# Batch 1's second softmax and first layer in one piece instead of two, with the order of the work searched anew

## The chip, the cores and the metric

The kernel runs on one core of one Trainium2 chip. The metric is the device time of one execution in microseconds; the median of a few runs is given. The profile shows one execution of the program, and its span runs from the first to the last instruction on the core.

## What is computed

An attention in two steps over 8 batches with 8 heads, 576 tokens and a head size of 64, in which 32 packed queries per head first gather the keys and values and the tokens then attend to the 32 gathered rows, and a two-layer network with a squared relu on the 4608 x 512 result (x). w_in is 512 x 2048 and w_out 2048 x 512.

```python
def sm_attn(qq, kk, vv):
    s = scale * np.matmul(qq, kk.transpose(0, 1, 3, 2))
    s = s - np.max(s, axis=-1, keepdims=True)
    a = np.exp(s)
    a = a / (np.sum(a, axis=-1, keepdims=True) + 1e-09)
    return np.matmul(a, vv)
p_packed = sm_attn(p, k, v)
out = sm_attn(q, p_packed, p_packed)
...
h = x @ w_in
r = np.maximum(h, 0.0)
g = r * r
return (g @ w_out).astype(np.float32)
```

## The kernel before, in words

The work goes batch by batch (b = 0 to 7), with 4 heads packed into the 128 partitions, so that each batch has two "quads" of heads (`qd`). For each batch:

- k is loaded, transposed (piece `Tk`, L741) and multiplied with p (`S1`, L774); its softmax is taken (`MX` L793, `EX` L801), transposed and multiplied with v (`PV`, L821), normalised (`XN`, L830), and transposed (`XQ`, `XM`, `XC`). This gives the packed rows.
- The packed rows are multiplied with w_in beforehand (`M`, L851, evicted by `MC`, L647 or L649), so that the second attention's output and the first layer need one product only: a2 (the softmax of the second scores) times M.
- q is loaded and transposed (`Tq`, L738) and multiplied with the packed rows (`S2`, L868) into PSUM. The second softmax works on a layout where the 32 columns of a token lie in a row: transposition out of PSUM (`SI`, L889), maximum (`SM`, L895), subtraction (`SU`, L899), exponential on ScalarE (`SE`, L902), sum and reciprocal (`SS`, L905 and L906), multiplication (`SN`, L912), transposition into a2 (`SO`, L916). All of these but `SE` are on VectorE.
- The first layer is M times a2: 16 blocks of 128 features. A relu from PSUM into bf16 and a square into gT follow, each on ScalarE or VectorE as the planner chooses.
- The second layer takes tiles of 128 tokens. Tiles 0 to 8 (and 13, 22 and 31) are plain sums over the 16 blocks (`F2`, L979; 31 is `FZ`, L997); the others are done in groups of four tiles by a Strassen step (`GP`, L1046), with sums of the weights (`WS`, L1024, eight instructions in all) and of the activations (`GS`, L1031) formed on VectorE. Tiles 0 to 3 need batch 0 alone, tile 4 needs batches 0 and 1, tiles 5 to 8 need batch 1.

Two batches differ from this. `PARTS` (L573) cuts the tokens of a batch for the second softmax and the first layer. A part is a pair: how many times 32 tokens it has, and how many feature blocks one first-layer group takes.

```python
PARTS = {0: ((4, 4), (6, 4), (8, 2)), 1: ((8, 2), (10, 2))}
def parts(b):
    return PARTS.get(b, ((8, 0), (10, 0)))
```

Batch 0 has parts of 128, 192 and 256 tokens. Batch 1 has parts of 256 and 320 tokens. A batch that is in `PARTS` takes each step from `SM` to `SO` once for every part (`SN` even once per quad of heads), and its first layer once for every part (pieces `F.1.x.j`, `R.1.x.j`, `Q.1.x.j`; `fh_mm` L953, `fh_relu` L961 or L963, `fh_sq` L971 or L973; two feature blocks to a group). A batch that is not in it takes the softmax over all 576 tokens at once (`steps`, L1177) and the first layer in 16 blocks of two times 288 tokens (pieces `F1`, `R`, `SQ`; `f1_mm` L925, `f1_relu` L935 or L937, `f1_sq` L943 or L945, the square over two blocks at a time). The score matmuls `S2` and the transposition `SI` are in two parts (256 and 320 tokens) for batches 1 to 4 either way; batches 5 to 7 use a DMA transposition and another form.

The order is set by a planner (`Plan.forward`, L70) that runs when the program is built. Every piece has an engine (or a choice of ScalarE and VectorE), an assumed duration, pieces that it waits for, and PSUM or buffer slots that it takes. The planner steps through an assumed time; whenever an engine is free, it starts the ready piece with the smallest priority. The priority is the level of the piece in the code (10 b + 2 for the second softmax of batch b, 30 + 10 t / 4.5 for second-layer tile t, 45 for the weight sums) plus a number from the table `TABLE['o']`; `TABLE['l']` shifts the choice between ScalarE and VectorE. Each engine then executes its instructions in the planned order. Before the first second-layer matmul, idle time that the plan sees on TensorE is filled with dummy matmuls (`keep_clock`, L653), which keep the clock up.

The loads run in a fixed order (`ORDER`) on the GpSimd queue, eight in flight at a time: the ninth is issued when the first has landed. Only batch 0's k, the p rows of batches 2 to 7 (L673, issued behind `XQ.1`) and the stores use the SyncE queue; the first p rows use ScalarE's. Batch 2's first scores `S1.2` need those p rows (`P.1` L680, `PT.1` L683).

PSUM has three pairs of banks (`PAIRS`) for scores, M and first-layer blocks, and four single banks for transpositions and second-layer tiles.

Of the kernel before, what the change touches and what calls it, by code (L numbers as in the profile page):

```python
# [14 lines left out]
P = 128  # L15
# [26 lines left out]
class Plan:  # L42
# [185 lines left out]
TABLE = {'o': {'Lk.0.0i': 134.746555333, 'Lk.0.1i': 23.540356465, 'Lk.0.0': 2.551236235, 'LP.0': 181.100529118,  # L228
# [330 lines left out]
def kernel_impl(tc, q, k, v, p, w_in, w_out, out):  # L559
    nc = tc.nc  # L560
    B, H, S, Dh = q.shape
# [11 lines left out]
    PARTS = {0: ((4, 4), (6, 4), (8, 2)), 1: ((8, 2), (10, 2))}  # L573
# [866 lines left out]
```

## Time and profile before

| | us |
|---|---|
| median of 3 runs (lowest, highest) | 236.37 (235.14, 236.86) |
| the profiled execution | 235.5 |
| its span | 233.7 |
| TensorE busy, 95% of the span | 221.5 |
| VectorE busy, 85% | 199.0 |
| ScalarE busy, 65% | 150.8 |
| GpSimd busy, 24% | 56.7 |

The profiled execution is 0.9 us under the median and within the three runs. A busy TensorE is not TensorE at its peak, since matmuls overlap and their ends are modelled; what is read below are its idle times and the spacing of matmuls. A row that gives "idle before" names what ended the wait. Where a row stands for several instructions, its count is behind the x.

### The profile page before, as it was taken

What the parts mean: (1) busy time and instruction counts of PE and PEld (TensorE: products, weight loads), DVE (VectorE), ACT (ScalarE), POOL (GpSimd) and SP (SyncE); (2) the same over time, 40 slices, a digit from 0 to 9 for tenths busy, and PEclk for the clock granted to TensorE, in tenths of its full rate; (3) what the DMA queues carried; (4) which work ended last, traced back from release to release, by engine and by line L of the source; (5) the groups of instructions that cost most, each with busy time, mean ns of one, the idle gap of its engine ahead of it and who ended that gap; (6) DMA issues with size and microseconds to landing.
All of it is one profiled execution on the core that took longest, in us unless ns stands there. A gap on an engine that the chain in (4) does not pass through costs nothing.

```text
span 233.7 us, 6367 instructions
## 1 busy us (share of the span) xinstructions
PE 221.5 (95%) x2615; PEld 159.8 (68%) x2631; DVE 199.0 (85%) x333; ACT 150.8 (65%) x246; POOL 56.7 (24%) x101
## 2 busy tenths in 40 slices
PE   8868999999999999999999999999999999999991
PEld 5644675455554467678767877887678878888880
DVE  3659887998899989999999999999999999479330
ACT  3334985388675888983997847749977917295100
POOL 9774445333344655630000000000000000000000
PEclk9999999999999999999999999999999999999998
DMA  6999999999999999999962969654241006106125
GB/s 234 189 150 206 205 207 203 202 204 262 221 224 214 228 229 194 174 134 153 207 140 63 157 78 210 157 101 97 56 92 45 1 3 147 36 0 140 42 56 168
DMA packets 46620, 34.06 MB, mean 146 GB/s; under 512 B 25280, under 2 KB 38336, under 8 KB 46592
## 3 DMA queue, kind: packets, MB, share of 16 engines
q0 software_dynamic: 19360, 18.03, 48.7%
q1 hardware_dynamic: 26384, 15.11, 30.2%
q10 hardware_dynamic: 848, 0.52, 1.0%
q8 instruction: 20, 0.33, 0.5%
q14 instruction: 8, 0.07, 0.1%
HBM read 37.22 MB, written 9.44 MB: 200 GB/s over the span
## 4 chain that ended last, share of the span: by engine, by line
PE 73%; DMA 21%; POOL 2%; issue 1%; DVE 1%; ACT 0%; POOLq 0%
PE ps L1046 32%; PE ps L925 21%; PE ps L979 9%; DMA w_out_b<-in_moe_w_out_dram 8%; DMA kq_b<-in_q_dram 6%; DMA w_in_b<-in_moe_w_in_dram 3%; PE ps L851 3%; DMA v_b<-in_v_dram 3%; PE ps L953 2%; PE ps L997 2%; PE ps L821 1%; PE ps L868 1%; PE ps L807 1%; PE ps L774 1%; POOL v_b L662 1%
## 5 line engine op out<-in xcount | busy, mean ns | idle before, releaser
L935 ACT ACTIVATE r_b<-ps 128x576 bf16<-128x576 f32 x84 | 49.5, 659 | 14.9 <-PE ps L925 14.7
L925 PE MATMUL ps<-a,M 128*128 128x288 bf16 x384 | 52.6, 286 | 0.2
L925 PEld LDWEIGHTS <-M 128*128 128x128 bf16 x384 | 37.2, 98 | 11.2 <-DVE a L916 0.3
L979 PE MATMUL ps<-w_out_b,gT 128*128 128x512 bf16 x160 | 41.3, 379 | 0.9 <-issue 0.3
L1046 PEld LDWEIGHTS <-gT 128*128 128x128 bf16 x384 | 36.7, 98 | 7.5 <-issue 3.1
L647 ACT CAST M<-ps 128x1024 bf16<-128x1024 f32 (+1 forms) x33 | 29.4, 932 | 16.5 <-PE ps L851 16.4
L1046 PEld LDWEIGHTS <-gS 128*128 128x128 bf16 x288 | 27.8, 98 | 4.1 <-DVE gS L1031 0.4
L991 POOL DMA_DIRECT2D out_dram<-o_sb x2 | 1.1, 571 | 120.1 <-DVE o_sb L1066 119.0
L945 DVE TENSOR_TENSOR gT<-r_b 128x1152 bf16<-128x1152 bf16 x38 | 27.8, 750 | 2.1 <-ACT r_b L935 2.0
L1066 DVE TENSOR_TENSOR o_sb<-o_sb,ps 128x512 f32<-128x512 f32 x30 | 20.2, 674 | 10.1 <-PE ps L1046 10.1
L647 ACT COPY o_sb<-ps 128x512 f32<-128x512 f32 (+1 forms) x24 | 13.7, 573 | 21.4 <-PE ps L997 9.5
L979 PEld LDWEIGHTS <-gT 128*128 128x128 bf16 x176 | 16.2, 98 | 14.7 <-issue 1.7
L1046 PE MATMUL ps<-w_out_b,gT 128*128 128x256 bf16 x192 | 24.1, 273 | 0.0
L1046 PE MATMUL ps<-wS,gT 128*128 128x256 bf16 x192 | 23.6, 273 | 0.0
L1046 PE MATMUL ps<-wS,gS 128*128 128x256 bf16 x192 | 23.6, 273 | 0.0
L953 PE MATMUL ps<-a,M 128*128 128x256 bf16 (+3 forms) x160 | 19.1, 262 | 1.4 <-DVE a L916 0.5
L953 PEld LDWEIGHTS <-M 128*128 128x128 bf16 x160 | 13.7, 98 | 7.3 <-issue 1.4
L961 ACT ACTIVATE r_b<-ps 128x512 bf16<-128x512 f32 (+2 forms) x28 | 16.9, 645 | 2.6 <-PE ps L953 2.5
L801 ACT ACTIVATE e<-ps,n 128x576 bf16<-128x576 f32 x16 | 11.8, 739 | 7.3 <-DVE n L793 7.2
L653 PE MATMUL ps<-o_sb 128*128 128x256 bf16 x90 | 13.5, 312 | 1.1 <-DVE o_sb L656 1.1
L793 DVE TENSOR_REDUCE n<-ps 128x1 f32<-128x576 f32 x16 | 11.6, 748 | 1.9 <-PE ps L774 1.9
L851 PE MATMUL ps<-w_in_b,ppT 64*32 64x512 bf16 x256 | 11.8, 382 | 0.6 <-DMA w_in_b<-in_moe_w_in_dram 0.4
(77 smaller groups left out, 317.6 us busy)
## 6 DMA issues: line engine op xcount, KB each, us to landing
out_dram<-o_sb SPq DMA_DIRECT2D x66, 128.0 KB, 2.7
kq_b<-in_k_dram POOLq DMA_DIRECT2D x14, 288.0 KB, 10.3
kq_b<-in_q_dram POOLq DMA_DIRECT2D x10, 288.0 KB, 6.4
w_out_b<-in_moe_w_out_dram POOLq DMA_DIRECT2D x8, 256.0 KB, 9.5
v_b<-in_v_dram POOLq DMA_DIRECT2D x5, 320.0 KB, 10.9
w_in_b<-in_moe_w_in_dram POOLq DMA_DIRECT2D x6, 256.0 KB, 9.1
v_b<-in_v_dram POOLq DMA_DIRECT2D x12, 128.0 KB, 8.8
v_b<-in_v_dram POOLq DMA_DIRECT2D x5, 256.0 KB, 10.6
```

The lines of the kernel that those rows point to most:

```text
L647: nc.scalar.copy(dst, src)
L653: nc.tensor.matmul(half(7)[:, :2 * P], lhsT=zero[:, :P], rhs=zero, start=True, stop=True)
L801: nc.scalar.activation(e_out(qd) if b in XBAR else e1[:, qd, :S], ps1[b, qd], ACT.Exp, bias=n1[b % 2][:, qd:qd + 1], accum_out=d1[b % 2][: ...
L851: nc.tensor.matmul(half(u[qd])[o:o + 32], lhsT=ppT[b % 2][r, 0, w:w + 32], rhs=w_in_b[r, h, c * WCH:(c + 1) * WCH], start=True, stop=True)
L925: nc.tensor.matmul(t[:, c], lhsT=M[b % 2][:, qd, fb * FB:(fb + 1) * FB], rhs=a2[b % 2][:, qd, c * HALF:(c + 1) * HALF], start=(qd == 0), s ...
L935: nc.scalar.activation(dst, src, ACT.Relu)
L945: eng.tensor_tensor(out=dst, in0=r, in1=r, op=ALU.mult)
L953: nc.tensor.matmul(t[:, c, m * w:(m + 1) * w], lhsT=M[b % 2][:, qd, fb * FB:(fb + 1) * FB], rhs=a2[b % 2][:, qd, o:o + w], start=(qd == 0) ...
L961: nc.scalar.activation(dst, ph["h", b, x, j], ACT.Relu)
L979: nc.tensor.matmul(po[t], lhsT=gT[:, fb, n0:n0 + P], rhs=w_out_b[:, fb, :], start=(fb == 0), stop=(fb == NFB - 1))
L1046: nc.tensor.matmul(pz[g, k][:, i], lhsT=a[:, f, i * P:(i + 1) * P], rhs=w[:, f], start=(k not in ON and h == 0 and f == 0 and i == 0), sto ...
L1066: nc.vector.tensor_tensor(out=oC(g, i, j), in0=oC(g, *src), in1=pz[g, z], op=ALU.add)
```

## The change

Batch 1 leaves `PARTS`, so its softmax runs as one step `SM.1` to `SO.1` over all 576 tokens, and its first layer as `F1.1`, `R.1`, `SQ.1` in the form that batches 2 to 7 have. The loop that collects which old readers of gT a square must wait for starts at tile 0 for batch 1, since its lower end would be negative. The whole table of priorities is replaced by one from a new search; no number of the old one is left. The load order, the number of loads in flight, the levels and the assumed durations are unchanged. The table is cut here to the lines that the text speaks of.

```diff
-TABLE = {'o': {'Lk.0.0i': 134.746555333, 'Lk.0.1i': 23.540356465, 'Lk.0.0': 2.551236235, 'LP.0': 181.100529118,
...
-    -215829.171971075, 'Tq.1.0': -215836.299950953, 'Tq.1.1': -215836.159754564, 'S2.1.0': -215742.74613255, 'SI.1.0':
-    -215809.783335566, 'S2.1.1': -123.135431214, 'SI.1.1': -215887.868645433, 'SM.1.0': -215837.962536453, 'SU.1.0':
...
-    -98.847449822, 'R.7': -216220.904415717, 'SQ.7': 15.825334762, 'WS.0': -105.983631041, 'WS.1': -215822.145212738,
...
+    -227633.226075536, 'Tq.1.1': -227818.777851646, 'S2.1.0': -227803.391094858, 'SI.1.0': -227640.638779293,
+    'S2.1.1': -29.276762611, 'SI.1.1': 0.247864716, 'SM.1': -35.475087001, 'SU.1': 0.062323842, 'SE.1':
+    -227793.881602248, 'SS.1': -1.13524686, 'SN.1': -11.918678126, 'SO.1': -227747.641802885, 'F1.1':
+    -227559.074732372, 'R.1': -227601.044985046, 'SQ.1': -227761.277447022, 'Tk.2.0': -20.244271561, 'Tk.2.1':
+    -5.304391657, 'S1.2': -227627.575072156, 'MX.2.0': -227691.281260216, 'EX.2.0': -227774.943262701, 'E.2.0':
...
+    -226566.920342397, 'R.7': -48.777700523, 'SQ.7': -48.549465201, 'WS.0': 74.467599958, 'WS.1': -227768.4863999,
+    'WS.2': -227677.207564371, 'WS.3': -227430.705855732, 'GS.0.2': -227565.136627528, 'GS.1.2': -227543.937748088,
...
+    'ST.34.1': -227656.084821736, 'ST.35.0': -227665.271932616, 'ST.35.1': -227443.171144139, 'F2.0':
+    -227893.454497088, 'FC.0': -227725.933670247, 'ST.0': -5.762464259, 'SD.0': -0.354082132, 'F2.1': -18.274953014,
...
+    -227748.02498843, 'ST.2': -227269.280746945, 'SD.2': 59.928635681, 'F2.3': -227883.79603422, 'FC.3': -2.955816309,
...
@@ kernel_impl
-    PARTS = {0: ((4, 4), (6, 4), (8, 2)), 1: ((8, 2), (10, 2))}
+    PARTS = {0: ((4, 4), (6, 4), (8, 2))}
...
                     old = [] if fb % 2 == 0 else old
-                    for t in range((b - 2) * S // P, ((b - 1) * S + P - 1) // P):
+                    for t in range(max(0, (b - 2) * S // P), ((b - 1) * S + P - 1) // P):
                         if t not in group_of:
                             old.append(f"F2.{t}.{fb}")
                             continue
```

More of the change, by code (lines that the diff above doesn't have):

```diff
@@ L226 @@
 XTURN = (5, 6, 7)
-TABLE = {'o': {'Lk.0.0i': 134.746555333, 'Lk.0.1i': 23.540356465, 'Lk.0.0': 2.551236235, 'LP.0': 181.100529118,
[328 rows of a table removed]
+TABLE = {'o': {'Lk.0.0i': -15.624462174, 'Lk.0.1i': 54.519872277, 'Lk.0.0': -117.982904162, 'LP.0': 56.853171331,
[304 rows of a table added]
 def kernel_impl(tc, q, k, v, p, w_in, w_out, out):
```

619 rows, old and new, of the table TABLE are left out of this document.

## The prediction

> **What bounds the kernel now.** I read five views of the profile: the busy times by stage, the chain that ended last, the order of time on TensorE around batch 1, the same on VectorE around batch 2 (whose second softmax is already whole), and the groups by shape. First the stages; the columns are the stretch in us, its length, and then busy time and instruction count of PE, PEld, DVE, ACT and POOL, the granted clock, and the DMA's share and rate.
>
> ```profile
> 0.00:25.00 25.00, 20.34 (x265) 13.79 (x266) 16.29 (x40) 10.10 (x20) 17.28 (x34) 1.00 1.08 196
> 25.00:40.00 15.00, 13.99 (x204) 9.71 (x205) 12.38 (x29) 12.19 (x24) 8.01 (x13) 1.00 1.23 204
> 40.00:50.65 10.65, 10.49 (x97) 4.20 (x91) 10.58 (x19) 6.01 (x9) 3.77 (x7) 1.00 1.23 197
> 50.65:67.40 16.75, 16.10 (x132) 10.04 (x135) 14.69 (x29) 13.87 (x26) 6.04 (x11) 1.00 1.17 241
> 67.40:84.00 16.60, 16.28 (x286) 8.32 (x288) 16.15 (x29) 11.81 (x21) 9.12 (x17) 1.00 1.25 217
> 84.00:228.50 144.50, 144.24 (x1651) 113.73 (x1654) 128.87 (x192) 96.44 (x150) 12.29 (x23) 1.00 0.60 107
> ```
>
> TensorE is idle for 1.01 us between 25 and 40, 0.16 us up to 50.65, 0.65 us up to 67.4, 0.32 us up to 84 and 0.26 us in the 144.5 us after that: 2.4 us in all after the start-up. Its amount of work does not change (below), so the end moves by what is added to or taken from those 2.4 us, and by what happens before 25 us. VectorE is nearly as full between 40 and 50.65 (10.58 of 10.65) but has 2.06 us free in the stretch after. The chain has one long wait inside the stage that changes:
>
> ```profile
> 40.94 14.76 DMA kq_b<-in_q_dram
> ...
> 55.72 0.79 DVE qT L738
> 56.51 0.51 DVE a L916
> ...
> 77.63 3.19 PE ps L979 x14
> ```
>
> The last step of part 1's softmax (L916) stood on VectorE behind a transposition of batch 2's q (L738), which itself waited for its load; TensorE waited 0.49 us for it, the gap in the second of the next rows. The last row above gives a second-layer matmul as 3.19 / 14 = 0.228 us. Now TensorE in order of time (start, duration, line, shape, count, idle time before):
>
> ```profile
> 39.60 0.42 PE L868 MATMUL ps<-qT,pq 32*32 32x256 bf16 x16
> ...
> 43.53 0.47 PE L868 MATMUL ps<-qT,pq 32*32 32x320 bf16 x16
> ...
> 50.65 1.04 PE L953 MATMUL ps<-a,M 128*128 128x256 bf16 x8
> ...
> 57.06 0.49 PE L953 MATMUL ps<-a,M 128*128 128x256 bf16 x3 [0.49 <-DVE a L916]
> ...
> 63.76 0.70 PE L774 MATMUL ps<-kT,pT 32*32 32x512 bf16 x32
> ...
> 71.47 0.70 PE L868 MATMUL ps<-qT,pq 32*32 32x256 bf16 x32
> ...
> 83.66 0.65 PE L925 MATMUL ps<-a,M 128*128 128x288 bf16 x4
> ```
>
> Batch 1's second scores (L868) come at 39.60 and 43.53, and its first layer starts at 50.65, when only the 256 tokens of part 0 are ready. For batch 2 the same way, unsplit, runs from 71.47 to 83.66: 12.19 us. What TensorE did in between is in the matmuls of L979 (second layer) by stretch; before 25 us there are none:
>
> ```profile
> 25.00:40.00 15.00, 4.86 (x18) 1.85 (x22) 1.00 1.23 204
> 40.00:50.65 10.65, 9.11 (x40) 3.62 (x41) 1.00 1.23 197
> ```
>
> Tiles 0 to 3 need only batch 0 and make 4 x 16 = 64 such matmuls. 58 are done by 50.65, so 6 are left, 6 x 0.228 = 1.4 us: without any of batch 1's first layer, TensorE would have run out of this work at about 52.0 us. That is the cover on which all depends.
>
> **The change part by part.** *Work on TensorE.* Before: 16 blocks x 2 halves of d x (256 + 320) columns. After: 16 x 2 x 2 x 288. Both are 16 x 2 x 576 columns with as many matmuls (64), so nothing is added. The second scores and their transposition keep two parts. Cost 0.
>
> *Work on VectorE and ScalarE.* The squares of batch 1 go from 8 of 128x512 and 8 of 128x640 to 8 of 128x1152:
>
> ```profile
> L945 DVE TENSOR_TENSOR gT<-r_b 128x1152 bf16<-128x1152 bf16 x38 | 27.8, 750 | 2.1 <-ACT r_b L935 2.0
> ...
> L973 DVE TENSOR_TENSOR gT<-r_b 128x512 bf16<-128x512 bf16 x13 | 4.9, 403 | 1.0 <-ACT r_b L961 1.0
> ...
> L973 DVE TENSOR_TENSOR gT<-r_b 128x640 bf16<-128x640 bf16 x5 | 2.4, 488 | 0.9 <-ACT r_b L961 0.9
> ...
> L912 DVE TENSOR_TENSOR n<-e,r 128x256 bf16<-128x256 bf16 x4 | 1.5, 436 | 0.0
> ...
> L912 DVE TENSOR_TENSOR n<-e,r 128x320 bf16<-128x320 bf16 x2 | 0.9, 504 | 0.0
> ```
>
> On VectorE that is 8 x (0.403 + 0.488) - 8 x 0.750 = 1.1 us less. The multiplication L912 was two instructions for each part, 2 x 0.436 + 2 x 0.504 = 1.88 us, and becomes one of 1.45 us (the row at 81.24 below): 0.4 us less. So some 1.5 us or a little more leave VectorE. TensorE is the full engine, so I count this as 0 at the end; the gain it could bring is bounded by TensorE's idle time after 50.65, 0.65 + 0.32 + 0.26 = 1.2 us.
>
> *The start of batch 1's first layer.* This is the term that can hurt: now nothing of it starts before all 576 tokens are through. The start of the stage is held by a load and cannot move earlier with the same load order: the second transposition of q ran at 38.20 with no idle time to make up, right as its piece came in. How long the whole way takes is shown by batch 2 on VectorE (and once on ScalarE):
>
> ```profile
> 72.51 1.41 DVE L889 STREAM_TRANSPOSE s<-ps 128x512 f32<-128x512 f32 x2
> ...
> 73.95 1.35 DVE L895 TENSOR_REDUCE m<-s 128x36 f32<-128x1152 f32 x1
> 75.22 1.43 DVE L738 STREAM_TRANSPOSE qT<-kq_b 128x576 f32<-128x576 f32 x2
> 76.57 1.32 DVE L899 TENSOR_TENSOR s<-s,m 128x1152 f32<-128x1152 f32 x1
> ...
> 79.44 1.35 DVE L905 TENSOR_REDUCE t<-e 128x36 f32<-128x1152 bf16 x1 [0.22 <-ACT e L902]
> 80.82 0.38 DVE L906 RECIPROCAL r<-t 128x36 f32<-128x36 f32 x1
> ...
> 81.24 1.45 DVE L912 TENSOR_TENSOR n<-e,r 128x1152 bf16<-128x1152 bf16 x1
> ...
> 82.78 0.76 DVE L916 STREAM_TRANSPOSE a<-n 128x576 f32<-128x576 f32 x1
> ```
> ```profile
> 78.24 1.17 ACT L902 ACTIVATE e<-s 128x1152 bf16<-128x1152 f32 x1
> ```
>
> The chain alone is 1.41 + 1.35 + 1.32 + 1.17 + 1.35 + 0.38 + 1.45 + 0.76 = 9.2 us; the rest of the 12.19 us are foreign instructions between its steps, such as the 1.43 us at 75.22. Three estimates from these rows for the first layer's start: 39.60 + 9.2 = 48.8 if nothing comes between; 39.60 + 12.19 = 51.8 if as much comes between as in batch 2; and, if the second score matmuls stay at 43.53, 43.53 + 0.47 + 0.7 (half of the 1.41) + 7.8 (the chain from the maximum on) + 2.0 (of batch 2's 3.0 us of foreign work what comes behind the maximum) = 54.5. The new table speaks for the middle: the table's smaller number goes first, and the weight sums WS.0 and WS.1, which VectorE did in the midst of the old softmax, stand behind all of it (45 + 74.5 = 119.5 for WS.0, on which WS.1 waits), as does the second transposition of batch 2's k (20 - 5.3 = 14.7 against 12.1 and less for the softmax); WS.2 stays ahead. The second scores (12 - 29.3 = -17.3) still stand behind tiles 0 and 3 of the second layer but ahead of tile 1 (32.2 - 18.3 = 13.9). I take 51.8, nearest to the batch 2 row, plus half a microsecond for what that row can't show: 52.3. The cover ends at 52.0: a wait of 0.3 us, between 0 and 2.5.
>
> *No other cover.* Batch 2's first scores (63.76 above) can't fill in earlier than about 52.7: they need the second part of p, whose load is issued at 38.13 and takes 14.6 us.
>
> ```profile
> 38.13 0.39 SPq L673 DMA_DIRECT2D wS<-in_p_dram x1
> ...
> wS<-in_p_dram SPq DMA_DIRECT2D x1, 384.0 KB, 14.6
> ```
>
> *The wait at 56.57 goes.* There is no part 1 any more that comes late behind batch 2's q: -0.49 us. Late next is nothing in this stage: once the whole of batch 1 is ready, its 64 matmuls can be streamed, as batch 2's are from 83.66 on, in a stretch whose idle time is 0.26 us in 144.5. If the first relus and squares had no cover, one of each would be the price (0.75 us for the square above and a relu of half its width taken as no longer, so at most 1.5 us); I take 0.
>
> *The new order elsewhere.* Batch 0 and the late batches keep their instructions, the load order and the eight loads in flight, so I take 0. Bounds: 1.0 us better, since that is TensorE's idle time from 25 to 40, and as much worse; from 67.4 on 0.6 us better, and 1.2 us worse if the weight sums moved back collide there.
>
> Sum: 0.3 - 0.49 + 0 + 0 = -0.2 us on the profiled execution of 235.5 us (span 233.7 and 1.8 around it). The three runs have a median of 236.37, 0.9 above that execution. So I predict 236.2 us, no change that a measurement can tell (about 1%, 2.4 us, is what can be told apart here).
>
> **The rivals.** *Late softmax (slower).* VectorE puts the M casts, squares of batch 0 and k transpositions between the steps, and the first layer starts at 54.5 or later. For: VectorE has 0.07 us free from 40 to 50.65. Against: the weight sums leave that stretch. TensorE waits 2.5 us and up to 1.5 us for the first relu and square: -0.49 + 2.5 + 1.5 = +3.5, some 239.9 us. It decides from a start at about 54.9 on, where the wait passes 2.4 + 0.49 us.
>
> *The same with the clock falling (slower).* After the last matmul the granted clock is still full for 2.5 us and then half; and the first matmuls that warm the clock take 5.69 / 28 = 0.203 us each against 1.37 / 11 = 0.125 later.
>
> ```profile
> 228.50:231.00 2.50, 0.02 (x1) 0.00 (x0) 0.00 (x0) 0.37 (x1) 0.15 (x1) 1.00 0.86 242
> 231.50:233.70 2.20, 0.00 (x0) 0.00 (x0) 0.00 (x0) 0.00 (x0) 0.00 (x0) 0.50 0.14 43
> ...
> 1.08 5.69 PE L653 MATMUL ps<-o_sb 128*128 128x256 bf16 x28 [1.08 <-DVE o_sb L656]
> ...
> 7.32 1.37 PE L653 MATMUL ps<-o_sb 128*128 128x256 bf16 x11
> ```
>
> A wait of 3 us or more in mid-kernel would then be followed by some 5 us at that rate, as at the start, which loses 5 x (1 - 0.125 / 0.203) = 1.9 us: 3.5 + 1.9 = +5.4, about 241.8 us. The Trainium skill, TensorE: Matmul & The Clock Gate, section HAM oscillation, says that the clock is throttled when TensorE is idle for more than about 3.4 us. The trace agrees at its end (still full 2.5 us after the last matmul, half from 3.0 us on); no wait in the middle of this trace is long enough to show it.
>
> *Everything earlier (faster).* The softmax runs undisturbed (start at 48.8) and the new order of batch 0 lets TensorE finish its cover that early too. Then 52.0 - 48.8 = 3.2 us go at most: 233.2 us. For: VectorE's removed 1.5 us and the moved sums. Against: the stretch before 40 us is held by loads that do not change.
>
> *VectorE is the hidden bound.* If its saving passes through, -1.2 more: 235.0, within 1% as well.
>
> **How the numbers follow.** Forecast (236.2, its own range 234.4 to 238.4, by the bounds of its terms: -0.2 - 1.0 - 0.6 = -1.8 and -0.49 + 2.5 = +2.0): 0.52. VectorE passing through: 0.04. Late softmax: 0.22. With the clock: 0.06. Everything earlier: 0.16. So faster by over 1% 0.16, within 1% 0.56, slower by over 1% 0.28. The range runs from 233.0 to 240.2: it holds the first two cases, a little over half of the faster one and three quarters of the late one, and leaves out 0.07 + 0.06 + the clock's 0.06 = 0.19.
>
> **What would show it.** Right: the first L925 row of batch 1 starts at 51 to 53 us; TensorE's idle time from 40 to 67.4 stays under 1.2 us; no L953 row follows batch 0; the stretch after 84 us keeps under 0.5 us idle. Wrong: a wait on L916 of over 2 us in that stretch, a granted clock under 1.00 before 228 us, weight sums late enough that L1046 waits for wS, or a TensorE idle time from 25 to 40 us far from 1.0.

## The result and the profile after

The changed kernel takes 238.29 us (median of 19 runs, 235.90 to 240.11), the kernel before 235.84 (19 runs, 234.99 to 237.51). The ratio is 1.0072, interval 1.0042 to 1.0101. The ratios here leave out executions that took over 1.5% longer than the fastest of the same kernel (one of these 19), so they need not be the quotient of the medians. The forecast was 236.2, 0.2 us less than the kernel before. The time lies inside the range, but the change loses about 1.7 us (by the ratio) to 2.45 us (by the medians), where the sum said that it gains a little.

The profiled execution took 238.67 us with a span of 236.9, 3.2 us more than the span before. Its stages, with the columns of the stage table of before:

```profile
0.00:25.00 25.00, 20.66 (x263) 14.10 (x263) 15.47 (x40) 10.99 (x20) 18.06 (x34) 0.93 1.07 196
25.00:40.00 15.00, 13.94 (x193) 9.73 (x204) 14.25 (x32) 11.50 (x22) 7.68 (x12) 1.00 1.23 204
40.00:50.65 10.65, 10.44 (x103) 4.41 (x105) 10.14 (x12) 5.99 (x8) 3.99 (x7) 1.00 1.23 198
50.65:67.40 16.75, 16.54 (x141) 10.48 (x141) 16.50 (x27) 11.58 (x21) 5.66 (x11) 1.00 1.17 234
67.40:84.00 16.60, 15.79 (x282) 7.32 (x291) 15.10 (x25) 10.70 (x20) 8.35 (x16) 1.00 1.25 224
84.00:142.00 58.00, 57.52 (x716) 43.58 (x726) 54.11 (x82) 45.78 (x76) 11.79 (x22) 1.00 1.02 154
142.00:147.00 5.00, 4.46 (x133) 2.94 (x128) 4.99 (x10) 3.79 (x8) 0.00 (x0) 1.00 0.48 106
147.00:157.00 10.00, 8.46 (x136) 6.59 (x134) 8.01 (x13) 5.42 (x7) 0.00 (x0) 1.00 0.76 153
157.00:180.00 23.00, 22.79 (x223) 16.64 (x223) 22.73 (x31) 15.37 (x22) 0.00 (x0) 1.00 0.39 82
```

The same late stretches of the kernel before, which the prediction had only as one long row:

```profile
84.00:142.00 58.00, 57.84 (x737) 43.19 (x738) 56.38 (x87) 45.28 (x74) 11.30 (x21) 1.00 0.95 152
142.00:147.00 5.00, 5.00 (x117) 4.18 (x109) 5.00 (x8) 3.18 (x4) 0.00 (x0) 1.00 0.98 193
147.00:157.00 10.00, 10.00 (x122) 7.98 (x120) 9.97 (x16) 6.42 (x10) 0.00 (x0) 1.00 0.59 124
157.00:180.00 23.00, 22.89 (x242) 17.09 (x242) 22.82 (x34) 19.49 (x31) 0.00 (x0) 1.00 0.37 80
```

Subtract the busy time of TensorE from the length of each stretch, before against after. In the stage of batch 1's first layer (50.65 to 67.4) this leaves 0.65 and 0.21 us, from 67.4 to 84 it leaves 0.32 and 0.81, from 84 to 142 0.16 and 0.48, and between 142 and 157, far from batch 1, 0 and 0.54 + 1.54 = 2.08 us. Not all of this is waiting. The profile of the kernel before has 160 matmuls of the second layer (L979) but 176 of their weight loads, that of the changed kernel (L955) 158 and 176. The other matmuls are missing from the profiles, and each leaves a gap of about 0.05 or 0.16 us that counts as idle. A second profile of the changed kernel (below) has them all, and there the long stretch is full:

```profile
84.00:142.00 58.00, 58.00 (x721) 43.57 (x724) 54.10 (x83) 45.77 (x76) 11.70 (x22) 1.00 1.04 154
```

Without these gaps, TensorE waits behind 40 us once in the kernel before, the 0.49 us at 57.06. In the changed kernel that wait is gone; instead there are 0.49 us between 70 and 72 us and 2.08 us between 142 and 157. So behind 40 us the change costs 2.08 of the 3.2 us by which the spans differ. The other 1.1 us come from the ends: at 40 us TensorE is some 1.4 us further behind with its work (by the end of its last matmul less the waits), after a stretch at half the granted clock (19.5 to 22.9 us), and what follows its last matmul is 0.3 us shorter.

TensorE in order of time, in the changed kernel (start, duration, line, shape, count, idle time before; its line numbers are 24 lower than before's):

```profile
39.94 0.70 PE L844 MATMUL ps<-qT,pq 32*32 32x256 bf16 x32
...
44.74 7.51 PE L955 MATMUL ps<-w_out_b,gT 128*128 128x512 bf16 x33
...
52.09 3.13 PE L901 MATMUL ps<-a,M 128*128 128x288 bf16 x24
...
70.08 0.23 PE L816 MATMUL ps<-ident,pp 128*128 128x128 bf16 x1 [0.38 <-DVE pp L806]
...
145.40 0.44 PE L854 MATMUL ps<-qT,ppT 64*32 64x288 bf16 x16
...
146.38 0.41 PE L827 MATMUL ps<-w_in_b,ppT 64*32 64x512 bf16 x8 [0.54 <-ACT ppT L623]
...
153.16 0.29 PE L854 MATMUL ps<-qT,ppT 64*32 64x288 bf16 x1
...
154.99 0.43 PE L854 MATMUL ps<-qT,ppT 64*32 64x288 bf16 x15 [1.54 <-DMA qT<-kq_b]
```

Batch 1's first layer starts at 52.09, right behind 33 second-layer matmuls, with no wait. Its softmax had ended 0.3 us before, on VectorE:

```profile
51.08 0.73 DVE L892 STREAM_TRANSPOSE a<-n 128x576 f32<-128x576 f32 x1
```

What is new stands further down in the rows of TensorE: the second scores of batch 6 (L854 at 153.16) stop after one matmul for 1.54 us, until a DMA has written qT. SyncE's queue shows why that DMA is late; first the changed kernel, with the link of its chain of waits that holds this DMA,

```profile
145.38 2.56 SPq L789 DMA_TRANSPOSE e<-e  x1
148.13 3.13 SPq L723 DMA_TRANSPOSE qT<-kq_b  x2
```
```profile
149.98 4.96 DMA qT<-kq_b
```

and then the kernel before, its queue and its two second scores of batches 5 and 6:

```profile
141.25 2.77 SPq L747 DMA_TRANSPOSE qT<-kq_b  x2
...
153.75 1.37 SPq L813 DMA_TRANSPOSE e<-e  x1
```
```profile
139.71 0.44 PE L878 MATMUL ps<-qT,ppT 64*32 64x288 bf16 x16
...
154.42 0.44 PE L878 MATMUL ps<-qT,ppT 64*32 64x288 bf16 x16
```

qT is one buffer, so batch 6's q can be written only after batch 5's second scores have read it. In the new order these scores moved from 139.71 to 145.40, 5.7 us later, and batch 7's e transposition was put ahead of the q transposition on the same queue. So the q transposition is issued at 148.13 and not at 141.25, 6.9 us later, while its reader comes 1.3 us earlier (153.16, not 154.42). Before, some 8 us lay between the landing and the use; now there is nothing.

The other new wait, 0.54 us at 146.38, is for ppT. ScalarE in the changed kernel:

```profile
143.59 0.75 ACT L777 ACTIVATE e<-ps,n 128x576 bf16<-128x576 f32 x1
...
144.32 0.74 ACT L777 ACTIVATE e<-ps,n 128x576 bf16<-128x576 f32 x1
...
145.04 1.02 ACT L623 CAST M<-ps 128x1024 bf16<-128x1024 f32 x1
145.93 0.40 ACT L623 COPY ppT<-ps 128x256 bf16<-128x256 bf16 x1
```

The 0.40 us copy that TensorE needs stands behind two exponentials of batch 7, which were moved up, and a cast. Between 67 and 75 us it is VectorE that is held up by a load, and the normalisation pp that TensorE waits for stands behind it (in the kernel before, this transposition of k came only behind pp, at 71.17):

```profile
69.07 0.78 DVE L717 STREAM_TRANSPOSE kT<-kq_b 128x576 f32<-128x576 f32 x1 [1.08 <-DMA kq_b<-in_k_dram]
69.77 0.25 DVE L806 TENSOR_TENSOR pp<-ps,r 128x128 bf16<-128x128 f32 x1
```

### The profile page after: what moved, and what is told of

Its sections match the earlier page's. It is cut to its first block, busy times and chain, and to the rows that moved or that the text cites. A ratio compares the mean times of both kernels' runs of the same rounds, so it can differ in the third digit from the quotient of the medians.

```text
span 236.9 us, 6358 instructions
## 1 busy us (share of the span) xinstructions
PE 222.6 (94%) x2614; PEld 160.6 (68%) x2632; DVE 200.1 (84%) x322; ACT 146.5 (62%) x240; POOL 57.2 (24%) x102
## 4 chain that ended last, share of the span: by engine, by line
PE 68%; DMA 13%; DVE 11%; issue 3%; ACT 2%; POOL 1%; SPq 0%; DVEq 0%; POOLq 0%
PE ps L1022 29%; PE ps L901 20%; PE ps L955 8%; DMA kq_b<-in_k_dram 5%; PE ps L827 3%; DMA v_b<-in_v_dram 3%; DMA kq_b<-in_q_dram 3%; PE ps L929 2%; DMA qT<-kq_b 2%; DVE wS L1000 2%; PE ps L973 1%; DVE t L881 1%; DVE n L888 1%; DVE s L865 1%; PE ps L844 1%
## 5 line engine op out<-in xcount | busy, mean ns | idle before, releaser
L911 ACT ACTIVATE r_b<-ps 128x576 bf16<-128x576 f32 x103 | 58.6, 657 | 18.1 <-PE ps L901 18.0
L901 PE MATMUL ps<-a,M 128*128 128x288 bf16 x448 | 60.1, 286 | 0.2
L901 PEld LDWEIGHTS <-M 128*128 128x128 bf16 x448 | 43.7, 98 | 12.6
L955 PE MATMUL ps<-w_out_b,gT 128*128 128x512 bf16 x158 | 41.3, 380 | 1.3 <-issue 0.8
L921 DVE TENSOR_TENSOR gT<-r_b 128x1152 bf16<-128x1152 bf16 x47 | 34.2, 749 | 4.7 <-ACT r_b L911 4.4
L623 ACT CAST M<-ps 128x1024 bf16<-128x1024 f32 (+1 forms) x31 | 27.3, 922 | 14.1 <-PE ps L827 14.0
L967 POOL DMA_DIRECT2D out_dram<-o_sb x3 | 1.7, 559 | 117.0 <-DVE o_sb L625 111.5
L955 PEld LDWEIGHTS <-gT 128*128 128x128 bf16 x176 | 15.9, 98 | 16.4 <-issue 2.2
L1022 PE MATMUL ps<-w_out_b,gT 128*128 128x256 bf16 x192 | 23.6, 273 | 0.2 <-issue 0.2
L629 PEld LDWEIGHTS <-o_sb 128*128 128x128 bf16 x91 | 9.7, 112 | 3.9 <-DVE o_sb L632 1.1
L888 DVE TENSOR_TENSOR n<-e,r 128x1152 bf16<-128x1152 bf16 (+3 forms) x13 | 11.8, 932 | 0.0
L1022 PE MATMUL ps<-w_out_b,gS 128*128 128x256 bf16 x96 | 11.8, 273 | 0.0
```

Of the source, the lines that this page charges most:

```text
L623: nc.scalar.copy(dst, src)
L629: nc.tensor.matmul(half(7)[:, :2 * P], lhsT=zero[:, :P], rhs=zero, start=True, stop=True)
L888: nc.vector.tensor_tensor(out=f(n2, "p (n i x) -> p n x i"), in0=f(e2, "p (n x i) -> p n x i"), in1=per(r2, o, w)[:, q].rearrange("p q n - ...
L901: nc.tensor.matmul(t[:, c], lhsT=M[b % 2][:, qd, fb * FB:(fb + 1) * FB], rhs=a2[b % 2][:, qd, c * HALF:(c + 1) * HALF], start=(qd == 0), s ...
L911: nc.scalar.activation(dst, src, ACT.Relu)
L921: eng.tensor_tensor(out=dst, in0=r, in1=r, op=ALU.mult)
```

## The experiments

Two theories were put to the test. Theory 1: leaving the split away costs nothing, and the loss is the new order of other work, above all behind 140 us. Theory 2: the whole softmax of batch 1 pushes all later batches back. To change one thing at a time, the order that the planner had found was written out as a list of starting times and used as the priority:

```diff
-        prio = [p.level + self.table.get("o", {}).get(p.key, 0.0) for p in ps]
+        prio = [AT[p.name] for p in ps]
```

### Only the split undone, old order (twice)

```diff
-    PARTS = {0: ((4, 4), (6, 4), (8, 2)), 1: ((8, 2), (10, 2))}
+    PARTS = {0: ((4, 4), (6, 4), (8, 2))}
+AT = {...}
```

The starting times are those of the kernel before, with batch 1's whole steps where its parts stood.

> Batch 1 in one piece as in the changed kernel, but every piece that both kernels have gets its place in the old kernel's plan as its priority; the one-piece softmax goes first on VectorE, and the first layer has the place of the old part 0. Theory 1 (not splitting costs nothing; the changed kernel loses its time through the new order of the start-up and of the late stage): as fast as before, between -0.5 and +0.7 us, TensorE idle from 84 us to its last matmul under 0.8 us, first layer of batch 1 from 50 to 53 us. Theory 2 (the one-piece softmax pushes all later batches back, and the late waits follow from it): as slow as the changed kernel, +1.5 to +3 us.

Measured: 236.81 us (8 runs), ratio 1.0058, 1.0034 to 1.0083, between what the two theories said. Behind 142 us no wait of TensorE is left. But in this profile the start-up came late: the second scores of batch 0 waited for q.

```profile
18.01 0.27 PE L868 MATMUL ps<-qT,pq 32*32 32x192 bf16 x4 [1.86 <-DVE qT L738]
```

So it was run again later.

> Batch 1 not split, all else in the order of the kernel before: the same kernel as in the first round, once more, since its 1.0058 is the one result that Theory 1 does not cover. If that loss is the start-up (the second piece of batch 0's q landed at 17.31 us in its profile, against 15.4 to 16.1 in the others), the time falls to that of before, ratio 0.999 to 1.003. If leaving the split away costs by itself, the ratio stays at 1.004 to 1.008, and the profile shows idle time of TensorE of about 0.5 us between 84 and 100 us again.

Measured: 235.89 us (12 runs), ratio 1.0024, 0.9996 to 1.0052. This is less than half of the first figure, though the two intervals overlap. What stayed in both profiles is idle time between 84 and 100 us, 0.46 us where before has no wait; the row is from the second one:

```profile
84.00:100.00 16.00, 15.54 (x223) 10.84 (x229) 15.03 (x25) 13.80 (x22) 9.00 (x17) 1.00 1.23 200
```

Under the old order, the two intervals leave anything from nothing to 0.8% as the cost of not splitting. By TensorE's waits it is nothing: against these 0.46 us stand the 0.49 us at 57 us, which are gone in both profiles.

### The new order, but with the split

```diff
-    PARTS = {0: ((4, 4), (6, 4), (8, 2))}
+    PARTS = {0: ((4, 4), (6, 4), (8, 2)), 1: ((8, 2), (10, 2))}
+AT = {...}
```

The starting times are those of the changed kernel, with batch 1's parts where its whole steps stood.

> The opposite pair: batch 1 split in two as before, every piece that both kernels have at its place in the changed kernel's plan, both parts' softmax first on VectorE, the 16 first-layer groups at the places of the 16 blocks. Theory 1: as slow as the changed kernel, within 0.7 us of it (+1 to +3 us against before), with the waits before the second scores of batch 6 still there. Theory 2: as fast as before, within 0.7 us.

Measured: 237.68 us (7 runs), ratio 1.0082, 1.0049 to 1.0115: as slow as the changed kernel, though batch 1 is split. The waits of TensorE from 135 to 185 us (line, who ended the wait, total us, times, longest):

```profile
PE ps L854 <- DMA qT<-kq_b: 1.6, 1, 1.6
PE ps L827 <- ACT ppT L623: 0.5, 1, 0.5
```

Both late waits are there. Theory 2 has fallen.

### The q transposition ahead of batch 7's e transposition

The changed kernel, with one piece taken out of its turn: each engine and queue gets its instructions in the order of this key.

```diff
-        for p in sorted(out, key=lambda p: p.start):
+        for p in sorted(out, key=lambda p: {'E.7': 146.5}.get(p.name, p.start)):
```

> The changed kernel with one step moved on SyncE's queue alone: the transposition of e for batch 7 is issued behind the two q transpositions of batch 6 instead of ahead of them; all other queues are the same. Theory 1: the q transpositions start about 2.2 us sooner (at 146 instead of 148.1 us), TensorE's wait of 1.5 us before the second scores of batch 6 is gone, and batch 7's product with v may wait up to 1 us instead: 0.5 to 1.5 us faster than the changed kernel. Theory 2: the wait only moves, since everything is late; within 0.3 us of the changed kernel.

Measured: 238.64 us (9 runs), ratio 1.009, 1.0057 to 1.0123. The gain did not come. Its profiled execution took 240.79 us, with the granted clock at half twice (18.9 to 22.3 and 155.4 to 158.8 us), so it is read for the waits alone:

```profile
PE ps L797 <- DMA e<-e: 2.5, 1, 2.5
```
```profile
146.72 2.75 SPq L723 DMA_TRANSPOSE qT<-kq_b  x2
...
150.01 1.32 SPq L789 DMA_TRANSPOSE e<-e  x1
```

The q wait is gone, and in its place TensorE waits 2.5 us for e, which landed 5.1 us after its issue. The q transposition moved up by only 1.4 us (148.13 to 146.72): that is the price of its place behind e. The other 5.5 us of its delay come from batch 5's second scores at 145.4, which hold qT. Two readers now stand close behind two transpositions of one queue, and either can come to wait.

### The old order, with only these transpositions late

```diff
-        for p in sorted(out, key=lambda p: p.start):
+        for p in sorted(out, key=lambda p: {'Tq.6.0': 147.2, 'Tq.6.1': 147.3}.get(p.name, p.start)):
```

> The old kernel with one step moved on SyncE's queue alone: the two q transpositions of batch 6 are issued behind the eight stores that followed them; all other queues are the same. Theory 1 (the place of these transpositions against the second scores sets a wait): they start 6 us later, at about 147 to 150 us, land at 153 to 157, and TensorE waits 0 to 3 us before the second scores of batch 6 (at 154.5 before); 0 to 3 us slower, by as much as the wait in its trace. Theory 2 (a late order alone costs little, there is slack behind it): within 0.5 us of before even where such a wait is seen.

Measured: 236.91 us (6 runs), ratio 1.0068, 1.0045 to 1.0092, with 0.9 us of waits for qT (the two transpositions landed 5.2 and 4.6 us after their issue):

```profile
PE ps L878 <- DMA qT<-kq_b: 0.9, 2, 0.6
```

The place of one pair of transpositions is enough to lose 1.1 to 2.2 us, about what the whole change loses.

### The two orders exchanged behind 122 us

First the changed kernel with the old order at the end: `AT` holds its own starting times up to about 122 us, and behind that those of the kernel before.

```diff
-        prio = [p.level + self.table.get("o", {}).get(p.key, 0.0) for p in ps]
+        prio = [AT[p.name] for p in ps]
+AT = {...}
```

> The changed kernel as it is (batch 1 not split, the newly searched order) up to about 122 us, and behind that point the work in the order of the kernel before: batch 6's q transposition ahead of batch 7's e transposition on SyncE's queue, the first layer of batch 5 and the output projections as before. Theory 1 (the loss comes from the order behind 140 us): the waits for batch 6's q (1.54 us) and for ppT (0.54 us) are gone, TensorE is idle less than 0.3 us between 142 and 157 us in place of 2.08, and the kernel takes 2.0 to 2.9 us less than the changed one, 235.4 to 236.5 us, a ratio of 0.998 to 1.003 to the kernel before (about 1 us of it may stay, lost between 67 and 75 us). Theory 2 (the whole softmax of batch 1 pushes the later batches back): nothing that happens behind 122 us is the cause, the time stays at 238.0 to 238.7, ratio 1.006 or more.

Measured: 235.92 us (12 runs), ratio 1.0006, 0.9977 to 1.0035. TensorE is never idle in the stretches where the changed kernel lost 2.08 us. The start-up goes out as the cause with it, since up to 122 us this kernel has the changed order, and its clock too stood at half (19.6 to 23.1 us):

```profile
142.00:147.00 5.00, 5.00 (x126) 3.69 (x125) 5.00 (x8) 3.44 (x4) 0.00 (x0) 1.00 1.02 206
147.00:157.00 10.00, 10.00 (x122) 7.99 (x121) 9.97 (x16) 6.42 (x10) 0.00 (x0) 1.00 0.55 116
```

Then the mirror, the kernel before (batch 1 split) with the new order at the end; one more line puts batch 7's e transposition ahead on the queue, as in the changed kernel:

```diff
-        prio = [p.level + self.table.get("o", {}).get(p.key, 0.0) for p in ps]
+        prio = [AT[p.name] for p in ps]
+AT = {...}
-        for p in sorted(out, key=lambda p: p.start):
+        for p in sorted(out, key=lambda p: {'Tq.6.0': 145.31}.get(p.name, p.start)):
```

> The mirror of the last round's exchange: the kernel before, batch 1 split and its own order up to about 122 us, and behind that point the changed kernel's order: batch 7's e transposition ahead of batch 6's two q transpositions on SyncE's queue, the second scores of batches 5 and 6 and the output projections as there. Theory 1 (the loss is the order behind 140 us, and nothing else is needed for it): waits of 1 to 2 us for batch 6's q and of about 0.5 us for ppT appear between 142 and 157 us, and the kernel takes 1.5 to 2.7 us more than before: ratio 1.006 to 1.011. Theory 2 (the unsplit softmax is needed for the loss): 0.998 to 1.002.

Measured: 237.52 us (10 runs), ratio 1.0088, 1.0055 to 1.0122. Its profile shows the ppT wait, but no wait of TensorE for qT:

```profile
PE ps L851 <- ACT ppT L647: 0.5, 1, 0.5
```

The profiled execution, 239.58 us, is the slowest of the ten. Some 3 us of its loss were there at 40 us already, behind a clock at half from 23.9 to 27.3 us; behind 122 us TensorE waits 1.2 us that the kernel before does not wait, the ppT wait and three others of 0.2 to 0.4 us.

Take the late order away and the loss goes; put it alone into the kernel before and the loss comes. Batch 1 in one piece is not needed for it. This rests on the times; in the mirror's one profile the waits behind 122 us make up about half of the 2 us that its median loses.

### A longer lag in the planner for this transposition

The priorities are the changed kernel's own starting times, as a list.

```diff
-        prio = [p.level + self.table.get("o", {}).get(p.key, 0.0) for p in ps]
+        prio = [AT[p.name] for p in ps]
+AT = {...}
-                    ... + quiet.get(b, issued[-1:]), lag=XLAG, level=L - 20)
+                    ... + quiet.get(b, issued[-1:]), lag=XLAG + 2.5 * (b == 6), level=L - 20)
```

> The changed kernel with one constant of the planner changed: from the end of batch 6's q transposition to the first use of what it wrote, the planner reckons with 2.5 us more; the plan's own priorities are kept. SyncE's queue is the same; only the place on TensorE of batch 6's second scores moves, behind output projections and the M products that were to follow them. Theory 1: the 1.54 us wait of these scores goes, since other products stand in their place, and the kernel takes 1 to 1.6 us less than the changed one: 236.7 to 237.3, ratio 1.003 to 1.006; the wait for ppT (0.54 us) stays. If instead the chain from batch 6's q over its second softmax to the end of the kernel is what sets the time, the idle time only moves to a later place on TensorE, and the ratio stays at 1.007 or more.

Measured: 236.96 us (6 runs), ratio 1.0079, 1.0052 to 1.0105. The median lies inside what was expected for the case that the wait goes (236.7 to 237.3), the ratio above it (1.003 to 1.006). The wait did go: batch 6's second scores start later and run through, the ppT wait stays.

```profile
145.60 0.41 PE L827 MATMUL ps<-w_in_b,ppT 64*32 64x512 bf16 x8 [0.54 <-ACT ppT L623]
...
155.56 0.44 PE L854 MATMUL ps<-qT,ppT 64*32 64x288 bf16 x16
```

So one wait is not the whole price of the late order: by the median some 1.4 us are left, by the ratio more. With six runs this experiment does not say where they are.

### A copy of the kernel before, and the changed kernel once more

The copy is the kernel before with its own starting times as priorities; nothing in its instructions differs.

> The kernel before, with its planned order written out as a list of starting times; every engine and queue issues the same instructions in the same order as in the kernel before. It prices what building the same work twice moves. If medians of five rounds here are good to 0.3%, the ratio lies between 0.997 and 1.003 (235.1 to 236.5 us against 235.8). If the old order without the split (1.0058 in the last round) lost its 1.4 us only to the start-up, in which the second piece of batch 0's q may land anywhere between 15.4 and 17.3 us, then a copy of the same instructions can lose as much: up to 1.006.

Measured: 235.66 us (12 runs), ratio 1.0012, 0.9987 to 1.0036. That is how far two equal kernels lie apart here. Its profile also shows a harmless case of two things that the changed kernel's profile has: a granted clock that falls to half at 20 to 22 us, and a q transposition that takes 5.0 us (the last row counts the four q transpositions from 130 to 170 us, shortest, median and longest time to landing).

```profile
20.00:22.00 2.00, 2.00 (x19) 1.03 (x18) 2.00 (x5) 0.89 (x2) 0.90 (x3) 0.50 1.26 212
```
```profile
DMA to landing us min/median/max: 3.2/3.4/5.0
```

This execution took 235.65 us, so here neither shows in the time.

> The changed kernel once more, for a second profile and for times in this round: ratio 1.004 to 1.010. Its runs fell into two groups before, 235.9 to 237.1 us and 237.7 to 240.1. If the groups differ by the late stage (batch 6's q, 1.54 us, and ppT, 0.54), a profile near 236 us shows those waits shorter by about as much; if they differ by the start-up, the late waits are the same in both and the first product of batch 0's second scores, or the granted clock before 25 us, differs.

Measured: 237.44 us (12 runs), ratio 1.0069, 1.0037 to 1.0101. Its runs again fall into two groups, six up to 237.15 and six from 237.72. The profiled one took 237.15, and its second scores of batch 6 run through:

```profile
153.15 0.56 PE L854 MATMUL ps<-qT,ppT 64*32 64x288 bf16 x16
```
```profile
DMA to landing us min/median/max: 3.2/3.3/3.4
```

It has a longer wait at another place, behind a k transposition for whose load VectorE waited 2.0 us:

```profile
70.27 0.23 PE L816 MATMUL ps<-ident,pp 128*128 128x128 bf16 x1 [1.32 <-DVE pp L806]
```

The first profile of the same kernel, 238.67 us, has for the same four transpositions:

```profile
DMA to landing us min/median/max: 3.2/3.3/5.0
```

The two executions are 1.5 us apart, and the q wait that one of them has is 1.54 us, but it does not explain the distance alone. The other waits 0.8 us longer at 70 us, so behind 40 us they differ by 0.7 us only; the rest lies before 40 us, where the clock fell to half in the first and not in the second. The second q transposition is issued at about 149.9 and read from 153.2 on: one that lands after 3.3 us is just in time, one that takes 5.0 is some 1.7 us late. Of the 31 runs of this kernel, 14 are at or below 237.15 us and 17 at or above 237.70. What sorts them is not shown: the landing of q, the load at 70 us and the start-up all differ between these two profiles. That a landing of 5.0 us brings the q wait is shown twice, here and by the split kernel in the new order (landing 5.0, wait 1.6).

### The kernel before with one exchange on VectorE (twice)

```diff
-        for p in sorted(out, key=lambda p: p.start):
+        for p in sorted(out, key=lambda p: {'SO.1.1': 53.925}.get(p.name, p.start)):
```

> The kernel before (batch 1 split as it was) with one change of order on VectorE alone: the 128 by 320 transposition of the normalised weights of batch 1's second part stands ahead of batch 2's first q transposition, and not behind it. If the wait of 0.49 us ahead of that part's first layer comes from this one q transposition (0.64 us) that stands in front, as the changed order suggests, the wait is gone, and the kernel takes 0.3 to 0.5 us less than before: ratio 0.998 to 0.999 if nothing comes back. If the q transposition that is now 0.3 us later is missed by batch 2's second scores at 70 us, the wait comes back there: ratio 1.000. Below the kernel-to-kernel scatter that the copy of the kernel before shows in this round, the profile alone tells the two apart.

> The kernel before with the one exchange on VectorE (the weights' transposition of batch 1's second part ahead of batch 2's first q transposition), once more, to see whether 0.9987 holds. If the 0.49 us wait ahead of that part's first layer went and nothing came back, the ratio is 0.998 to 0.999 again; if it was scatter between builds, as large as the 1.0012 of the copy of before, it lies anywhere from 0.998 to 1.002.

Measured: 235.25 us, ratio 0.9987 (0.9968 to 1.0006), and 235.10 us, ratio 0.9976 (0.9947 to 1.0006), 12 runs each. VectorE in the first of them, and the first-layer matmul that had waited 0.49 us:

```profile
54.82 0.51 DVE L916 STREAM_TRANSPOSE a<-n 128x320 f32<-128x320 f32 x1
55.25 0.74 DVE L738 STREAM_TRANSPOSE qT<-kq_b 128x576 f32<-128x576 f32 x1
```
```profile
57.36 0.71 PE L953 MATMUL ps<-a,M 128*128 128x320 bf16 x4
```

The wait is gone, with the split in place; the first profile has a new one of 0.3 us nearby (second-layer matmuls at 58.35, for gT), the second has none. Twice the result is 0.1 to 0.2% faster, as 0.3 to 0.5 us would be, and twice the interval just takes in 1: the fastest version of this study, by less than can be called certain.

## Why the prediction was wrong, point by point

**What bounds the kernel.** Right: TensorE's idle time is the account in which the change shows. 2.08 of the 3.2 us between the two spans are waits of TensorE behind 40 us. But part of what it counted as idle is matmuls missing from the profile: of the 0.65 + 0.32 + 0.26 = 1.2 us behind 50.65 only the 0.49 us at 57.06 are a wait.

**Work on TensorE, 0.** Right within the noise: under the new order the kernel with the split (1.0082) and without it (1.0072, 1.0069) cannot be told apart; under the old order it is 1.0058 and, in the repeat, 1.0024.

**Work on VectorE and ScalarE, 0 at the end.** Right at the end, for another reason than the one given. The 1.5 us did not leave VectorE, by the page of the changed kernel:

```profile
PE 222.6 (94%) x2614; PEld 160.6 (68%) x2632; DVE 200.1 (84%) x322; ACT 146.5 (62%) x240; POOL 57.2 (24%) x102
```

VectorE is at 200.1 (199.0 before), and ScalarE has fallen from 150.8 to 146.5. The sum had all sixteen squares of batch 1 on VectorE. In the kernel before, nine of them ran there and seven on ScalarE; in the changed kernel seven of the eight whole squares run on VectorE, some 1.2 us more and not 1.1 less. The unsplit kernel in the old order shows the same (199.3 and 147.5 in its repeat).

**The start of batch 1's first layer, 52.3 against a cover to 52.0.** Right, in part by luck: 52.09, and no wait. The softmax was through at 51.81, where batch 2's row had put it (51.8). The cover was miscounted: 58 matmuls up to 50.65 are in the profile, but 61 of the 64 weight loads start before that, so 3 matmuls or 0.7 us were left and the cover ended near 51.3. In the changed kernel it lasted to 52.09 because TensorE came later to this work (59 loads by 50.65).

**The wait at 56.57 goes, -0.49.** Right: it is gone, here and in both profiles of the unsplit kernel in the old order. Leaving the split away is not the only thing that removes it, though: the exchange on VectorE does so too.

**The new order elsewhere: "Batch 0 and the late batches keep their instructions, the load order and the eight loads in flight, so I take 0".** This is the step that failed. That the instructions stay says nothing of their order, and the order is what the change replaced. It bounded the loss behind 67.4 us at 1.2, for weight sums that collide; the profile shows waits of 0.49 + 2.08 = 2.57 us there, 2.08 of them behind 142 us, and none is for a weight sum. And it could be read before the run: the number of batch 5's second scores in the table goes from -215729.39 to -2.98, from among the pieces that go first to about its level. These scores free qT, and the next q transposition waits for them. The prediction read the new numbers of batch 1 and of the weight sums only, and of SyncE's queue not a row. The range did not take in its own bounds of 1.0 and 1.2 us worse either; its slow end came from the late softmax, which did not come, so that 238.29 lies inside is luck.

**The rivals.** The late softmax did not come: 52.09, not 54.9. The clock did fall, though not for its reason: it is at 0.93 before 25 us, and a copy of the kernel before with the same fall is no slower. "VectorE is the hidden bound" had nothing to pass on, since VectorE did not get less work. "Everything earlier" did not come either. The case that happened, a wait made by the new order far away from batch 1, was not among them.

**What would show it.** The list did hold the right test: idle time under 0.5 us behind 84 us. By the same reckoning it came out as 0.48 + 0.54 + 1.54 + 0.21 = 2.8 up to 180 us, 2.08 of them waits.

**What stays open.** How the price of the late order is made up. The ppT wait (0.46 to 0.54 us) is in every profile that has this order, the q wait only in those where a transposition lands late, and without the q wait some 1.4 us or more are still lost. Open too is what the k transposition ahead of pp costs: TensorE waits there from nothing to 1.32 us in the profiles with the new order. The changed kernel with the old order at the end keeps that part of the new order and loses nothing measurable; its one profile has no such wait.

## What to carry to other kernels

Where a change comes with a new search of the order, price the order first: compare, for each single buffer and each in-order queue, who writes, who reads and how much time lies between, for all batches and not only for the one that the change names. A transfer needs slack for its slow case, since a plan that leaves it just the usual time can turn each slow landing into a stall. Test such a change by exchanging one stretch of the order at a time, in both directions: that separates the edit from the search that came with it.

## What the runs showed of the hardware

- A DMA transposition of q (issued by SyncE, between 130 and 170 us) landed 3.2 to 3.6 us after its issue in most cases, but in 7 of the 14 profiles of this study at least one of the four took 4.9 to 5.2 us. The kernel before has 8 us between landing and use and does not show it; the changed kernel has none. The planner reckons with 1.6 + 2.9 = 4.5 us (`XUS`, `XLAG`), between the two.
- The granted clock fell to 0.50 between 18 and 28 us in 5 of the 14 profiles, for 3.4 us each time (the prediction had reckoned with 5). In the changed kernel and in the copy of before it fell after waits of TensorE of at most 1.05 and 1.76 us; in the profile of the unsplit kernel in the old order it stayed at 1.00, behind the wait of 1.86 us that is shown above. Once it fell in mid-kernel, 0.3 us after the wait of 2.5 us for e. The Trainium skill, TensorE: Matmul & The Clock Gate, section HAM oscillation, names idle gaps of more than about 3.4 us as what brings the clock down; here it fell without one, and did not fall behind a longer wait. At the end of the kernel before, too, it fell 2.9 us after the last matmul. What decides is not shown by these runs.
- Matmuls can be missing from a profile: 16 of 2631 in that of the kernel before, 18 of 2632 in the first of the changed kernel, none in the second. Each leaves a gap that looks like idle time; the weight loads of the same line are all there and tell the two apart.
